# A step takes one query block of all four batches and two pairs of heads

## The chip, the core and the metric

The kernel runs on one core of a Trainium2 chip. Its engines are TensorE (PE in the profile, its weight load PEld), VectorE (DVE), ScalarE (ACT), GpSimd (POOL) and SyncE (SP); each works through its own instructions in order. Here SP issues nearly all transfers between the chip's main memory and its on-chip memory, and sixteen DMA engines carry them out. The metric is the device time of one execution in microseconds (us).

## What is computed

Block-sparse attention over 4 batches, 8 heads, 768 positions in 24 blocks of 32, head size 64, and then a two-layer network over all 3072 positions:

```python
mask = np.abs(blk_i - blk_j) <= 1                       # the block and its two neighbours
mask = mask | (blk_i == 0) | (blk_j == 0) | (blk_i == n_blocks - 1) | (blk_j == n_blocks - 1)
for qb in range(n_blocks):
    for kb in sampled_blocks[qb]:                       # three random blocks for each query block
        mask[qb*block:(qb+1)*block, kb*block:(kb+1)*block] = True
scores = np.where(mask, scale * q @ k^T, -1e9)
attn = softmax(scores);  x = attn @ v                   # then heads side by side: 3072 x 512
h = x @ w_in;  out = (h - np.tanh(h)) @ w_out           # 512 -> 2048 -> 512
```

The first and the last query block see all 768 keys; each of the 22 others sees at most eight blocks: itself and its neighbours, the first, the last, and three sampled ones. The samples are the same in all batches and heads, and known only when the kernel runs.

## The kernel before

**Two stages.** The attention runs first, in 60 units; the network (`FFN`) follows, in 96 units of 512 rows by 128 hidden columns, and its first units overlap the last ones of the attention. Results of the attention go through memory (`xscr`) to the network.

**Units of the attention.** Each unit works on 128 partitions in four quarters of 32 query rows. A batch has 15 units: two pairs Y and X (`kind` "Y", "X"), in which blocks 0 and 23 of four heads go over all keys; ten "group" units, each four query blocks by two pairs of heads; and a "rest" for blocks 21 and 22. The batches follow each other. A unit has `scores` (PE), `most` (row maxima, DVE), `exps` (ACT), `turn` (transposes, PE), `copy` (DVE and ACT), `accum` (weights times V, PE) and `norm` (DVE, then the store of tile x to `xscr` by SP).

**Operands.** `kq` holds K and Q of one batch on chip, two batches at a time; `vnat` holds V of one batch in its natural order for X and Y. For the group units GpSimd copies the sampled columns of K into `kr` (`gather_k`: twelve copies of 128x128 for a group of four blocks, which two units share), and SP fetches rows of V into `vw` (`gather_v`): one transfer for the neighbours of four blocks (96 partitions, 780 KB) and twelve of one sampled block each (32 partitions, 65 KB; a row is 520 numbers, 2080 bytes). The first and last block's rows lie in partitions 96 to 127 and are fetched once a batch for each of the three `vw` buffers.

**What sets the order.** The order is written by hand: every part of unit n is given a time (`at(n + 2.6, accum, u)`), all are sorted, and each engine receives its instructions in that order. `gather_v` of a group stands just behind the `accum` that last read its `vw` buffer, some five units ahead of its own use. SP takes its list in order: a transfer that has to wait holds all behind it. Its transfers use eight completion semaphores in turn (DMAHW0 to DMAHW7 below), and each waits until the transfer eight places ahead of it has landed. Tile x has two buffers, in a pool that it shares with the network's tile u, so the `norm` of a unit writes x only after the store of two units before has landed.

**Weights.** They come as 64-bit words and are turned into 32-bit ones on DVE (`convert_op`); six of the 32 weight tiles are converted during the attention (`load_pre`, `convert_pre`).

Of the kernel before, what the change touches and what calls it, by code (L numbers as in the profile page):

```python
# [44 lines left out]
STEP = 15  # L45
TE = STEP * B + 1.9
LOADK, LOADV, PRE0, DPRE = 1.5, 7.2, 6.1, 6
X0, X1, STAGE = 47, 55.5, (54, 54.5, 56, 56.5)
# [7 lines left out]
NG = 6  # L56
# [37 lines left out]
def attention_ffn(ctx, tc, kq, v, samp, w_in, w_out, rows, out):  # L94
# [3 lines left out]
    xscr = [dpool.tile([S, DM], F32, name=f"xscr{b}") for b in range(B)]  # L98
# [23 lines left out]
class Unit:  # L122


    def __init__(self, n, kind, bt, g, c):
        self.n, self.kind, self.bt, self.g, self.c = n, kind, bt, g, c
        if kind == "group":
            self.quads = [(1 + 4 * g + q, q, None) for q in range(4)]
        elif kind == "rest":
            self.quads = [(21 + q % 2, q % 2, q // 2) for q in range(4)]  # L130
        else:
            self.quads = [((NB - 1) * (q % 2), None, q // 2) for q in range(4)]

    def pair(self, q, half):
        a = self.quads[q][2]
        if self.kind == "group":
            return 2 * self.c + half
        return 2 * (half if self.kind == "rest" else self.c) + a


def attention(ctx, tc, kq, v, samp, w_in, w_out, rows, xscr, ident, banks, mem, px, f2, ffn):
    nc = InOrder(tc)
    att = ctx.enter_context(tc.tile_pool(name="att", bufs=1))
    sm = ctx.enter_context(tc.tile_pool(name="sm", bufs=4))
    sbank, tbank, obank = banks[:4], banks[4:6], banks[6:]

    vw = [att.tile([P, 4, 2, VW], F32, name=f"vw{i}") for i in range(3)]
    kr = [att.tile([P, H // 2, 4, 160], F32, name=f"kr{i}") for i in range(2)]
    wraw = att.tile([P, 1024], I32, name="wraw")
    wtmp = att.tile([P, 256], I32, name="wtmp")  # L150
    vnat = [px.tile([P, 2 * S], F32, tag=("rawx", "rawx", "lo")[i], name=f"vnat{i}")[:, 0 : 2 * VW] for i in range(3)]
    vnat = [t.rearrange("p (t e) -> p t e", t=2) for t in vnat]
    kqs = {}

    def load_kq(bt):
        kqs[bt] = mem.tile([P, H // 2, 2, S], F32, tag=f"A{bt % 2}", name=f"kq{bt}")
        for p in range(H // 2):
            eng = nc.scalar if bt == 0 and p % 2 else nc.sync
            eng.dma_start(out=kqs[bt][:, p], in_=kq[bt][:, p])

    def load_vnat(bt):
        for i in range(3):
            nc.sync.dma_start(out=vnat[i], in_=v[bt][2 * P * i : 2 * P * (i + 1), :].rearrange("(t p) e -> p t e", p=P))
# [27 lines left out]
    def values(eng, x, g, top):  # L191
        n = 12 if g < 5 else 6
        ins, vals = tc.nc.values_load_multi_w_load_instructions(
            x[0:1, 12 * g : 12 * g + n], engines=[eng], min_val=0, max_val=top,
            skip_runtime_bounds_check_because="the samples are clamped into this range on the chip",
        )
        for i in ins:
            tc.keep_in_program_order(i)
        return vals

    def gather_k(bt, g):
        k, to = kqs[bt][:, :, 0, :], kr[g % 2]
        if g < 2:
            for b, c in ((0, 0), (NB - 1, 128)):
                nc.gpsimd.tensor_copy(
                    out=to[:, :, :, c : c + 32], in_=k[:, :, b * 32 : b * 32 + 32].unsqueeze(2).to_broadcast([P, H // 2, 4, 32])
                )
        for i, x in enumerate(values(mybir.EngineType.Pool, kx, g, S - 32)):
            o = 32 + 32 * (i % 3)
            nc.gpsimd.tensor_copy(out=to[:, :, i // 3, o : o + 32], in_=k[:, :, bass.ds(x, 32)])  # L210

    def gather_v(bt, g):
        to, b0, n = vw[g % 3], 1 + 4 * g, 4 if g < 5 else 2
        src = v[bt]
        e = nc.sync
        if g < 3:
            for b, c in ((0, 0), (NB - 1, 1)):
                rows = bass.AP(tensor=src.tensor, offset=src.offset + b * 32 * VW, ap=[[VW, 32], [0, 4], [1, VW]])
                e.dma_start(out=to[96:128, :, c, :], in_=rows)
        l0, l1 = int(g == 0), n - (g == 5)  # L220
        if l1 > l0:
            rows = bass.AP(tensor=src.tensor, offset=src.offset + (b0 + l0 - 1) * 32 * VW, ap=[[VW, 96], [32 * VW, l1 - l0], [1, VW]])
            e.dma_start(out=to[0:96, l0:l1, 0, :], in_=rows)
        if g == 0:
            e.dma_start(out=to[0:32, 0, 0, :], in_=src[S : S + 32, :])
            e.dma_start(out=to[32:96, 0, 0, :], in_=src[32:96, :])
        if g == 5:
            e.dma_start(out=to[0:64, 1, 0, :], in_=src[S - 96 : S - 32, :])
            e.dma_start(out=to[64:96, 1, 0, :], in_=src[S : S + 32, :])
        for i, x in enumerate(values(mybir.EngineType.SP, vx, g, S)):  # L230
            o = 32 * (i % 3)
            e.dma_start(out=to[o : o + 32, i // 3, 1, :], in_=src[bass.ds(x, 32), :])
# [4 lines left out]
    def scores(u):  # L237
        s = sbs[u.n] = sbank[2 * (u.n % 2) : 2 * (u.n % 2) + 2]
        t = kqs[u.bt]
        if u.kind in "XY":  # L240
            o = 0 if u.kind == "X" else 512
            w = 512 if u.kind == "X" else 256
            parts = [(0, slice(0, w), None, slice(o, o + w))]
        else:
            parts = [(h, slice(256 * h + o, 256 * h + o + w), x, None) for h in range(2) for x, o, w in (("w", 0, 96), ("r", 96, 160))]
        for h, cols, what, ks in parts:
            for q in range(4):
                b, l, _ = u.quads[q]
                p = u.pair(q, h)
                for j in range(2):  # L250
                    r = slice(64 * j, 64 * j + 64)
                    if what == "r":
                        rhs = kr[u.g % 2][r, p, l, :]
                    else:
                        rhs = t[r, p, 0, ks or slice(32 * b - 32, 32 * b + 64)]
                    mm(s[j][32 * q : 32 * q + 32, cols], t[r, p, 1, 32 * b : 32 * b + 32], rhs)
# [38 lines left out]
    def accum(u):  # L295
        o = obank[(u.n + (u.kind == "Y")) % 2]
        first = True
        for j in (1, 0):
            for h in (0, 1) if u.kind not in "XY" else (0,):
                chunks = range(2) if u.kind not in "XY" else range(4) if u.kind == "X" else (4, 5)  # L300
                for x, ch in enumerate(chunks):
                    for q in range(4):
                        _, l, _ = u.quads[q]
                        hd = 2 * u.pair(q, h) + j
                        t = pts[u.n, j][:, P * (2 * h + x) + 32 * q : P * (2 * h + x) + 32 * q + 32]
                        e = slice(65 * hd, 65 * hd + 65)
                        r = vnat[ch // 2][:, ch % 2, e] if u.kind in "XY" else vw[u.g % 3][:, l, ch, e]
                        c = slice(65 * (2 * h + j), 65 * (2 * h + j) + 65)
                        last = u.kind != "Y" and x == len(chunks) - 1
                        mm(o[32 * q : 32 * q + 32, c], t, r, start=first and u.kind != "X", stop=last)  # L310
                    first = False

    def norm(u):
# [5 lines left out]
        x = f2.tile([P, 512], F32, tag="u", name=f"x{u.n}")[:, 0 : 64 * n]  # L319
# [3 lines left out]
        to = xscr[u.bt]  # L323
        if u.kind == "group":
            r0 = 32 * (1 + 4 * u.g)
            nc.sync.dma_start(out=to[r0 : r0 + P, 256 * u.c : 256 * u.c + 256], in_=x)
        elif u.kind == "rest":
            for a in range(2):
                nc.sync.dma_start(
                    out=to[672:736, :].rearrange("q (c a d) -> q c a d", c=2, a=2)[:, :, a], in_=x[64 * a : 64 * a + 64].rearrange("q (c d) -> q c d", c=2)  # L330
                )
        else:
            for q in range(4):
                r0, c0 = 32 * u.quads[q][0], P * u.pair(q, 0)
                nc.sync.dma_start(out=to[r0 : r0 + 32, c0 : c0 + P], in_=x[32 * q : 32 * q + 32])
# [6 lines left out]
    at(-9, load_kq, 0)  # L342
    at(-8.9, load_samples)
    at(-8.8, load_vnat, 0)
    units = []
    for bt in range(B):
        for k in range(4):
            units.append(Unit(len(units), "YX"[k % 2], bt, None, k // 2))
        for g in range(5):
            for c in range(2):  # L350
                units.append(Unit(len(units), "group", bt, g, c))
        units.append(Unit(len(units), "rest", bt, 5, None))
    assert len(units) == STEP * B
    for u in units:
        n = u.n
        at(n + 0.3, scores, u)
# [16 lines left out]
    for bt in range(B):  # L373
        n = STEP * bt
        if bt:
            at(n - STEP + LOADK if bt > 1 else -8, load_kq, bt)
            at(n - STEP + LOADV, load_vnat, bt)
        for g in range(NG):
            at(n + 4 + 2 * g - 2.65, gather_k, bt, g)
            at(n + 4 + 2 * g - 2.35 if g > 2 or bt else -5 + g, gather_v, bt, g)  # L380

# [16 lines left out]
    ffn.room(1, mem.tile([P, 8 * S], F32R, tag="A2", name="flat1"))  # L398
    for k in range(2 * NPRE):
        t = PRE0 + DPRE * k  # L400
        at(t, load_pre, k)
        for e in range(2):
            for x in range(3):
                at(t + 2.4 + 1.5 * e + 0.5 * x, convert_pre, k, e, x)
        at(t + 5.12, convert_pre, k, 1, 3)
# [340 lines left out]
```

## Time and profile before

| | us |
|---|---|
| median of three runs (937.07 to 941.82) | 940.14 |
| the profiled execution | 937.58 |
| its span | 935.8 |
| last write of an attention result x | 406.81 |
| from there to the end of the span | 529.0 |

| engine | busy us | share of the span |
|---|---|---|
| PE | 771.4 | 82% |
| PEld | 622.3 | 67% |
| DVE | 566.7 | 61% |
| ACT | 439.5 | 47% |
| POOL | 267.0 | 29% |

The shares are means over two stages that have different limits, so they say little by themselves: the span is read in stretches. An engine's busy time leaves out the issuing of transfers and the waiting on semaphores; a row of a timeline or of the waits names behind "<-" what ended an idle time. KB in a row are units of 1024 bytes.

### The profile page before, as it was taken

To read this page: it belongs to the slowest core of one execution; us is meant where nothing else is said; L and a number is where in the kernel's file an instruction comes from. 1 tells how busy PE (TensorE), PEld (TensorE's weight loads), DVE (VectorE), ACT (ScalarE), POOL (GpSimd) and SP (SyncE) were. 2 spreads that over 40 slices of the span, in tenths; PEclk is the share of its full clock that TensorE was granted. 3 is DMA by queue.
4 is the path that set the end of the run, shared out by engine and by line. 5 is a ranking of instruction groups with operands and counts; after the bars stand their busy time and mean duration, and the time that the engine had idled before them with its cause. 6 is when DMAs were issued, how large, how long until landed. Compare 5 with 4: busy or idle time off the path is not lost.

```text
span 935.8 us, 23960 instructions
## 1 busy us (share of the span) xinstructions
PE 771.4 (82%) x9440; PEld 622.3 (67%) x9440; DVE 566.7 (61%) x1083; ACT 439.5 (47%) x843; POOL 267.0 (29%) x436
## 2 busy tenths in 40 slices
PE   2746855686448666599999999999999999999997
PEld 1535534564337455578888888888888888888886
DVE  3435622465236544469899668777667666766654
ACT  1323422244113342357877755555555555555453
POOL 3112311132113021037787422222222222222222
PEclk9878876688667897999999999999999999999999
DMA  9776576847775576614742110211201110001001
GB/s 353 180 210 154 200 166 149 222 129 231 175 194 133 149 179 181 192 41 135 209 142 89 45 28 8 65 25 26 68 0 17 26 50 1 0 1 46 1 1 45
DMA packets 92725, 99.84 MB, mean 107 GB/s; under 512 B 44995, under 2 KB 60356, under 8 KB 92612
## 3 DMA queue, kind: packets, MB, share of 16 engines
q1 hardware_dynamic: 92180, 96.47, 38.4%
q8 instruction: 74, 1.21, 0.6%
q10 hardware_dynamic: 432, 1.84, 0.5%
q14 instruction: 39, 0.32, 0.1%
HBM read 84.62 MB, written 13.63 MB: 105 GB/s over the span
## 4 chain that ended last, share of the span: by engine, by line
PE 63%; DMA 20%; SPq 8%; DVE 4%; issue 3%; ACT 1%; POOL 0%; DVEq 0%; ACTq 0%; POOLq 0%
PE ps L79 63%; DMA vw<-v 15%; SPq L79 8%; DMA xscr<-x 3%; DVE m L79 1%; DMA vnat<-v 1%; DVE pt L79 1%; DVE nb L79 1%; DVE x L79 0%; ACT p L79 0%; ACT flat L79 0%; DMA flat<-xscr 0%; POOL gl L79 0%; ACT pt L79 0%; DVE rs L79 0%
## 5 line engine op out<-in xcount | busy, mean ns | idle before, releaser
L79 POOL TENSOR_TENSOR gl<-t,gh 128x512 fp32r<-128x512 f32 x96 | 124.7, 1299 | 309.1 <-ACT gh L79 286.8
L79 PE MATMUL ps<-flat,wx 128*128 128x512 f32 x720 | 172.9, 389 | 0.0
L79 ACT ACTIVATE p<-ps,nb 128x256 f32<-128x256 f32 x208 | 89.7, 490 | 161.4 <-DVE nb L79 150.2
L79 PEld LDWEIGHTS ps<-flat,wx 128*128 128x128 f32 x720 | 135.2, 188 | 28.1
L79 ACT ACTIVATE u<-ps 128x512 f32<-128x512 f32 x96 | 57.5, 599 | 198.2 <-PE ps L79 196.3
L79 PE MATMUL ps<-wx,gh 128*128 128x512 f32 x480 | 147.8, 389 | 0.0
L79 PE MATMUL ps<-vw,pt 128*32 128x65 f32 x2816 | 68.8, 252 | 91.5 <-DVE pt L79 88.1
L79 POOL COPY kr<-kq 128x128 f32 (+1 forms) x280 | 73.5, 315 | 215.6 <-PE ps L79 201.8
L79 PEld LDWEIGHTS ps<-vw,pt 128*32 128x32 f32 x2816 | 59.8, 128 | 108.8 <-DVE pt L79 99.9
L79 DVE TENSOR_REDUCE m<-ps 128x2 f32<-128x512 f32 (+2 forms) x120 | 76.5, 649 | 59.8 <-PE ps L79 56.2
L79 DVE TENSOR_TENSOR t<-t,ps 128x512 f32<-128x512 f32 x74 | 50.7, 685 | 86.0 <-ACT t L79 86.0
L79 PEld LDWEIGHTS ps<-wx,gh 128*128 128x128 f32 x480 | 90.1, 188 | 18.6
L79 PE MATMUL ps<-ident,p 128*128 128x128 f32 x448 | 84.5, 347 | 11.1 <-DVE flat L79 4.4
L79 PE MATMUL ps<-wx,gl 128*128 128x512 f32 x240 | 93.4, 389 | 0.0
L79 PE MATMUL ps<-kq 64*32 64x96 f32 (+2 forms) x1664 | 58.1, 336 | 32.2 <-ACT p L79 19.9
L79 DVE TENSOR_TENSOR x<-ps,rs 128x256 f32<-128x256 f32 (+1 forms) x52 | 21.0, 404 | 104.0 <-DMA xscr<-x 102.4
L79 PEld LDWEIGHTS ps<-ident,p 128*128 128x128 f32 x448 | 65.9, 178 | 23.0 <-issue 6.2
L79 DVE COPY_PREDICATED t<-mk,ps 128x512 f32<-128x512 int32 x96 | 71.3, 743 | 7.5 <-DVE ps L79 0.9
L79 ACT ACTIVATE pt<-ps 128x512 f32<-128x512 f32 (+1 forms) x60 | 34.2, 570 | 88.0 <-PE ps L79 87.7
L79 DVE TENSOR_TENSOR ps<-ps,u 128x512 f32<-128x512 f32 x96 | 66.6, 694 | 11.6 <-ACT hs L79 11.5
L79 DVE SCALAR_TENSOR_TENSOR ps<-qq,ps 128x512 f32<-128x512 f32 x96 | 66.6, 694 | 7.7
L79 PE MATMUL ps<-kr,kq 64*32 64x160 f32 x1408 | 55.6, 349 | 18.3 <-issue 18.3
(82 smaller groups left out, 1189.0 us busy)
## 6 DMA issues: line engine op xcount, KB each, us to landing
vw<-v SPq DMA_DIRECT2D x272, 65.0 KB, 3.4
vw<-v SPq DMA_DIRECT2D x16, 780.0 KB, 8.5
kq<-kq SPq DMA_DIRECT2D x14, 768.0 KB, 8.6
stage<-w_in SPq DMA_DIRECT2D x13, 512.0 KB, 3.9
stage<-w_out SPq DMA_DIRECT2D x13, 512.0 KB, 3.3
vnat<-v SPq DMA_DIRECT2D x12, 520.0 KB, 7.3
vw<-v SPq DMA_DIRECT2D x24, 260.0 KB, 4.9
xscr<-x SPq DMA_DIRECT2D x40, 128.0 KB, 2.1
```

The lines of the kernel that those rows point to most:

```text
L79: r = f(*args, **kw)
```

## The change

A unit now takes one query block of all four batches, and two pairs of heads (`c`): the four quarters are the batches. The units of c = 0 come first, then those of c = 1; each half has four pairs Y and X (one for each batch) and 22 "block" units, 60 in all as before. The inputs are laid out for it on the host: K, Q and V by halves of the heads, and a row of V holds all four batches (1040 numbers, 4160 bytes).

- `gather_v` of a unit is one transfer of 96 rows (390 KB), into `vw[i][0]`, and three of 32 rows (130 KB each), into `vw[i][1]`; there are four such pairs of buffers, each for one unit. First and last block's rows are fetched once a half for each (`edges_v`, 130 KB).
- `gather_k` of a unit is three GpSimd copies of 128x256.
- `kq` is loaded by halves, all batches of c = 0 ahead of the first block unit; those of c = 1 during the units of c = 0, and so is `vnat`, now four tiles (rows of 1040 bytes).
- Tile x has a pool of its own with four buffers.
- `xscr` has one tile for each block (32 rows of each batch), so the network takes its rows block by block, and an output tile of 128 rows is stored by four transfers of 32 rows.
- The six early weight tiles are converted from unit 31 on (before: from unit 6 on), since their room is that of the first half's K and Q.

```diff
-STEP = 15
+STEP = 30
-LOADK, LOADV, PRE0, DPRE = 1.5, 7.2, 6.1, 6
-X0, X1, STAGE = 47, 55.5, (54, 54.5, 56, 56.5)
+NVW, NKR, VNAT = 4, 2, T * 260
+LOADK, LOADV, PRE0, DPRE = 9.5, 16, 31, 4
+X0, X1, STAGE = 44, 52, (54, 54.5, 56, 56.5)
...
-    vw = [att.tile([P, 4, 2, VW], F32, name=f"vw{i}") for i in range(3)]
-    kr = [att.tile([P, H // 2, 4, 160], F32, name=f"kr{i}") for i in range(2)]
+    xs = ctx.enter_context(tc.tile_pool(name="xs", bufs=4))
+    vw = [[att.tile([P, B, VW // 2], F32, name=f"vw{i}{x}") for x in range(2)] for i in range(NVW)]
+    kr = [att.tile([P, H, 160], F32, name=f"kr{i}") for i in range(NKR)]
...
+    def gather_v(u):
+        (wa, ra), src, b = vw[u.i % NVW], v[u.c], u.b
         e = nc.sync
...
+        e.dma_start(out=wa[lo:hi], in_=src[32 * b - 32 + lo : 32 * b - 32 + hi])
...
+        for i, x in enumerate(values(mybir.EngineType.SP, vx, b, S)):
+            e.dma_start(out=ra[32 * i : 32 * i + 32], in_=src[bass.ds(x, 32)])
...
-        x = f2.tile([P, 512], F32, tag="u", name=f"x{u.n}")[:, 0 : 64 * n]
+        x = xs.tile([P, 256], F32, tag="x", name=f"x{u.n}")[:, 0 : 64 * n]
...
+        if u.kind == "block":
+            nc.sync.dma_start(out=xscr[u.b][:, 256 * u.c : 256 * u.c + 256], in_=x)
...
+        if u.kind == "block":
+            at(n - NKR + 0.35, gather_k, u)
+            at(n - NVW + 2.65 if u.i >= NVW else -3.5, gather_v, u)
...
-            eng.dma_start(out=self.out[(CT * n + j) * P : (CT * n + j + 1) * P, :], in_=ob)
+            for bt in range(B):
+                r0 = S * bt + BLK * (CT * n + j)
+                eng.dma_start(out=self.out[r0 : r0 + BLK, :], in_=ob[BLK * bt : BLK * bt + BLK])
```

Three places of SP's list show what moved. In the rows, vw, kq, vnat and x are the tiles named above, and the name in square brackets is what the transfer waits for: a semaphore of the eight, or an engine.

The first place is in the middle of the attention, before: the end of one group's fetch, two stores of x and the start of the next fetch.

```order
L79 DMA vw_103<-v 32x520 [waits DMAHW4_49]
L79 DMA xscr_61<-x_2679 128x256 [waits DMAHW5_49,DVE_49]
L79 DMA xscr_61<-x_2775 128x256 [waits DMAHW6_49,DVE_49]
L79 DMA wraw<-w_out 128x1024 [waits DMAHW7_49]
L79 DMA vw_104<-v 96x4x520 [waits DMAHW0_49,PE_49]
L193 TENSOR_LOAD vx
L79 ISA
L79 DMA vw_104<-v 32x520 [waits DMAHW1_49,PE_49]
```

The same place in the changed kernel: the end of one unit's fetch, one store, and the next unit's whole fetch.

```order
L79 DMA vw_133<-v 32x1040 [waits DMAHW1_49]
L79 DMA xscr_64<-x_1251 128x256 [waits DMAHW2_49,DVE_49]
L79 DMA vw_126<-v 96x1040 [waits DMAHW3_49,PE_49]
L193 TENSOR_LOAD vx
L79 ISA
L79 DMA vw_127<-v 32x1040 [waits DMAHW4_49,PE_49]
L79 ISA
L79 DMA vw_127<-v 32x1040 [waits DMAHW5_49]
L79 ISA
L79 DMA vw_127<-v 32x1040 [waits DMAHW6_49]
L79 DMA xscr_65<-x_1402 128x256 [waits DMAHW7_49,DVE_49]
L79 DMA kq_173<-kq 128x3072 [waits DMAHW0_49]
```

Between two stores there stood thirteen fetches of one group, and now stand the four of one unit; K and Q of the second half come between them.

The second place is the head of SP's list, before:

```order
L79 DMA kq_116<-kq 128x1536 x2
L79 DMA si<-samp 1x144
L79 DMA ri<-rows 1x66
L79 DMA vnat_110<-v 128x2x520
L79 DMA vnat_111<-v 128x2x520
L79 DMA vnat_112<-v 128x2x520
L79 DMA kq_149<-kq 128x1536 x4
L79 DMA vw_103<-v 32x4x520 x2
```

And in the changed kernel:

```order
L79 DMA kq_144<-kq 128x1536
L79 DMA si<-samp 1x144
L79 DMA ri<-rows 1x66
L79 DMA vnat_138<-v 128x6x260
L79 DMA kq_144<-kq 128x3072
L79 DMA vnat_139<-v 128x6x260
L79 DMA kq_144<-kq 128x3072
L79 DMA vnat_140<-v 128x6x260
L79 DMA kq_144<-kq 128x3072
L79 DMA vnat_141<-v 128x6x260
L79 DMA vw_126<-v 32x1040
```

K, Q and V of four batches, for half of the heads, now stand ahead of the first fetch into vw; before it was K and Q of two batches and V of one, for all heads.

The third place is SP's end, the stores of the network's last four output tiles (one goes by ACT), before:

```order
L663 DMA out<-ob_0_11596 128x512
L663 DMA out<-ob_1_11599 128x512
L663 DMA out<-stage_6541 128x512
```

And in the changed kernel:

```order
L657 DMA out<-ob_0_10832 32x512 x4
L657 DMA out<-ob_1_10838 32x512 x4
L657 DMA out<-stage_5726 32x512 x4
```

Three stores have become twelve.

## Rows read from the trace of the kernel before

**Rows 1.** The page's slices, 40 of equal length: DMA share and GB/s.

```profile
DMA  9776576847775576614742110211201110001001
GB/s 353 180 210 154 200 166 149 222 129 231 175 194 133 149 179 181 192 41 135 209 142 89 45 28 8 65 25 26 68 0 17 26 50 1 0 1 46 1 1 45
```

**Rows 2.** Busy time by stretch: start:end, length, engines, PEclk, DMA share, GB/s.

```profile
12.40:56.50 44.10, 21.87 (x584) 15.32 (x584) 15.84 (x50) 13.04 (x27) 12.82 (x51) 0.87 0.85 231
57.00:407.00 350.00, 224.09 (x6519) 175.37 (x6520) 165.45 (x443) 113.23 (x256) 66.94 (x235) 0.79 0.66 174
407.00:936.00 529.00, 522.44 (x2306) 430.54 (x2305) 383.85 (x585) 313.24 (x561) 185.47 (x144) 1.00 0.17 47
```

**Rows 3.** The same view, short stretches in which one kind of transfer runs.

```profile
151.50:159.00 7.50, 5.70 (x136) 4.60 (x136) 3.11 (x10) 2.69 (x6) 0.88 (x1) 0.58 1.06 232
159.50:163.00 3.50, 0.00 (x0) 0.00 (x0) 0.00 (x0) 0.00 (x0) 0.00 (x0) 0.74 0.40 101
166.00:170.00 4.00, 3.89 (x72) 3.68 (x72) 2.78 (x9) 0.84 (x2) 0.00 (x0) 0.50 0.99 363
8.00:22.00 14.00, 4.32 (x48) 1.34 (x30) 7.02 (x26) 3.60 (x6) 7.03 (x24) 1.00 1.03 409
```

**Rows 4.** Timeline of SP, two groups: start, length, instruction, count.

```profile
150.11 11.84 SPq L79 DMA_DIRECT2D vw<-v  x15
162.05 2.23 SPq L79 DMA_DIRECT2D xscr<-x  x5
...
165.93 12.28 SPq L79 DMA_DIRECT2D vw<-v  x13
178.31 1.99 SPq L79 DMA_DIRECT2D xscr<-x  x2
...
180.87 4.42 SPq L79 DMA_DIRECT2D vw<-v  x7
```

**Rows 5.** Waits of the engines: who waited for whom, us, times, longest.

```profile
DVE x L79 <- DMA xscr<-x: 102.4, 18, 13.1
...
PE ps L79 <- DVE pt L79: 92.3, 29, 11.5
```

**Rows 6.** Waits of SP's own list, same columns.

```profile
SPq L79 <- DMA vw<-v: 48.8, 32, 3.5
```

**Rows 7.** GpSimd's copies into kr, by form: count, busy us, mean ns, idle.

```profile
L79 POOL COPY kr<-kq 128x128 f32 x264 | 64.5, 297 | 190.1 <-PE ps L79 186.2 <-issue 3.7
...
L79 POOL COPY kr<-kq 128x512 f32<-128x512 f32 x16 | 9.4, 617 | 25.5 <-PE ps L79 15.5 <-DMA kq<-kq 10.0
```

**Rows 8.** Transfers by kind: count, KB each, median us from issue to landing.

```profile
vw<-v SPq DMA_DIRECT2D x272, 65.0 KB, 3.4
vw<-v SPq DMA_DIRECT2D x16, 780.0 KB, 8.5
kq<-kq SPq DMA_DIRECT2D x14, 768.0 KB, 8.6
...
vnat<-v SPq DMA_DIRECT2D x12, 520.0 KB, 7.3
```

**Rows 9.** Timeline of DVE, writes of x: start, length; the last is the attention's last.

```profile
111.03 0.42 DVE L79 TENSOR_TENSOR x<-ps,rs 128x256 f32<-128x256 f32 x1
...
119.49 0.29 DVE L79 TENSOR_TENSOR x<-ps,rs 128x128 f32<-128x128 f32 x1 [0.27 <-DVE rs L79]
...
196.89 0.42 DVE L79 TENSOR_TENSOR x<-ps,rs 128x256 f32<-128x256 f32 x1
...
211.98 0.42 DVE L79 TENSOR_TENSOR x<-ps,rs 128x256 f32<-128x256 f32 x1
...
406.81 0.42 DVE L79 TENSOR_TENSOR x<-ps,rs 128x256 f32<-128x256 f32 x1
```

**Rows 10.** Timeline of SP at the end of the span.

```profile
930.73 0.81 SPq L663 DMA_DIRECT2D out<-ob  x2
931.65 0.38 SPq L663 DMA_DIRECT2D out<-stage  x1
```

More of the change, by code (lines that the diff above doesn't have):

```diff
@@ L55 @@
 VW = H * (D + 1)
-NG = 6
 THR2 = 0.16
@@ L97, in attention_ffn @@
     dpool = ctx.enter_context(tc.tile_pool(name="dpool", bufs=1, space=DRAM))
-    xscr = [dpool.tile([S, DM], F32, name=f"xscr{b}") for b in range(B)]
+    xscr = [dpool.tile([P, DM], F32, name=f"xscr{b}") for b in range(NB)]
     ident = cst.tile([P, P], F32, name="ident")
@@ L122, with __init__, at @@
 class Unit:
[L125 to L138, printed above, removed]
+    def __init__(self, n, kind, c, b, i=None):
+        self.n, self.kind, self.c, self.b, self.i = n, kind, c, b, i
+    def at(self, q, half):
+        if self.kind == "block":
+            return q, self.b, half
+        return self.b, (NB - 1) * (q % 2), q // 2
 def attention(ctx, tc, kq, v, samp, w_in, w_out, rows, xscr, ident, banks, mem, px, f2, ffn):
@@ L189, in load_samples @@
         e.tensor_scalar(out=kx, in0=sf, scalar1=float(BLK), scalar2=None, op0=ALU.mult)
[L191 to L210, printed above, removed]
@@ L212, in gather_v @@
-    def gather_v(bt, g):
-        to, b0, n = vw[g % 3], 1 + 4 * g, 4 if g < 5 else 2
-        src = v[bt]
-        e = nc.sync
[L216 to L232, printed above, removed]
+    vals = {}
@@ new lines, in values, with edges_k @@
+    def values(eng, x, b, top):
+        if b % 4 == 1:
+            ins, vals[eng] = tc.nc.values_load_multi_w_load_instructions(
+                x[0:1, 3 * b - 3 : min(3 * b + 9, 66)], engines=[eng], min_val=0, max_val=top,
+                skip_runtime_bounds_check_because="the samples are clamped into this range on the chip",
+            )
+            for i in ins:
+                tc.keep_in_program_order(i)
+        b = 3 * ((b - 1) % 4)
+        return vals[eng][b : b + 3]
+    def edges_k(c, i):
+        k = kqs[c].rearrange("p b a x s -> p (b a) x s")[:, :, 0, :]
+        for b, o in ((0, 0), (NB - 1, 128)):
+            nc.gpsimd.tensor_copy(out=kr[i][:, :, o : o + 32], in_=k[:, :, b * 32 : b * 32 + 32])
@@ L322, in norm @@
         )
[L323 to L331, printed above, removed]
+        if u.kind == "block":
+            nc.sync.dma_start(out=xscr[u.b][:, 256 * u.c : 256 * u.c + 256], in_=x)
         else:
             for q in range(4):
-                r0, c0 = 32 * u.quads[q][0], P * u.pair(q, 0)
-                nc.sync.dma_start(out=to[r0 : r0 + 32, c0 : c0 + P], in_=x[32 * q : 32 * q + 32])
+                bt, b, p = u.at(q, 0)
+                c0 = P * (2 * u.c + p)
+                nc.sync.dma_start(out=xscr[b][32 * bt : 32 * bt + 32, c0 : c0 + P], in_=x[32 * q : 32 * q + 32])
     ev = []
@@ L552, in fetch_x @@
         raw = self.raw[n, j] = raw if n == 2 and j == 3 else raw.bitcast(F32)
-        b, t = divmod(CT * n + j, T)
-        rows = self.xscr[b][t * P : (t + 1) * P, :]
+        rows = self.xscr[CT * n + j]
         if n < BLOCKED:
@@ L708, in rest @@
         wc = pool("wc")
-        self.tiles += [wc.tile([P, 512], F32R, name=f"wx{i}") for i in range(4 * (NFT - 6))]
+        self.tiles += [wc.tile([P, 512], F32R, name=f"wx{i}") for i in range(4 * (NFT - 6) - 12)]
         for t, f, args in sorted(self.ev, key=lambda e: e[0]):
```

141 lines of the change are left out of this document (79 added, 62 removed).

## The prediction

> **What bounds the kernel now.** I read the slices first [rows 1]: the DMA engines are 0.4 to 0.8 busy in the first 17 or 18 of 40 slices and nearly idle later. Then the busy times by stretch [rows 2]: from 57 to 407 us PE is busy 224 of 350 us and DVE 165, so no engine fills the stretch; from 407 on PE is busy 522 of 529 us. The last attention result is written at 406.81 us [rows 9]. The network behind it is bound by PE, and the change leaves its arithmetic alone; what can move is the attention.
>
> The DMA share there is only 0.66 [rows 2], but the short stretches [rows 3] show two rates of a full queue. Loads to all 128 partitions (kq, vnat) run at 409 GB/s (share 1.03) and 363 (0.99). Fetches into vw run at 232 GB/s with the engines just as full (1.06). Rows of V are 2080 bytes long in vnat and in vw alike, so the lower rate goes with the partitions that are reached (32 or 96), not with the length of a row. And when a group's wide transfer is gone and only its 65 KB pieces are left, the rate is 101 GB/s at share 0.40.
>
> That last figure is SP's own pace: seven issues in 4.42 us [rows 4] are 0.63 us each, and 66.6 kB in 0.63 us are 106 GB/s. So a group costs SP about 12 us (11.84 for fifteen transfers, 12.28 for thirteen) [rows 4], and with its stores 15 to 16 us pass from one group to the next (150.11, 165.93, 180.87), for two units. SP also waits 48.8 us on the landing of earlier vw transfers [rows 6]: with eight semaphores, the ninth transfer waits for the first, and the 780 KB one takes 8.5 us to land [rows 8]. The stores of x stand behind all this; DVE waits 102.4 us for them, and PE 92.3 us for DVE's pt [rows 5], since in DVE's list the copy of pt follows the blocked write of x. PE then frees the vw buffer late, and SP waits again: a ring of waits.
>
> How full is the queue? Fetches into vw are 40,560 KB, or 41.5 MB: 272 pieces and 16 wide ones [rows 8], the rest first and last rows and odd ends. At 232 GB/s they take 179 us. K, Q and V in full (19.0 MB) take 46 us at 409, stores, six weight tiles and early loads of x (11.5 MB) 28 us. Sum 253 us of the 404 from the first load to the last x: 0.63. When SP did nothing but load (12.4 to 56.5 us), the share was 0.85 [rows 2].
>
> **The change part by part.** *Bytes.* A unit fetches 390 + 3 x 130 = 780 KB, just what half a group did. With first and last rows (2 x 1040 KB) the halves make 37.3 MB instead of 41.5.
>
> *Rate.* A row is twice as long, but it goes to the same 32 or 96 partitions. No row shows 4160-byte rows there; the bounds are 232 GB/s (row length does nothing) and 363 (as to 128 partitions). I take 232, because 2080-byte rows reach both rates today.
>
> *SP.* A unit has four fetches and one store. At 0.63 us each these are 3.2 us, against 3.44 us (0.799 MB at 232) that the fetches need and 0.32 for the store; a piece of 133 kB in 0.63 us is 211 GB/s, twice today's pace. So SP no longer starves the queue. Eight transfers in flight are then 1.6 units, 1.5 MB.
>
> *Waits.* Four buffers of x, and a store after every fourth fetch instead of after thirteen, take away what DVE's 102.4 us wait on. The fetch of unit n is released by `accum` of unit n-4, so it has four steps to land. The depth falls from six units to four, but four steps of 4.8 us are 19 us, against landings of 3.4 to 8.5 us [rows 8]. If that cover went, PE would stand by the whole difference in each step.
>
> *Compute.* Where today nothing is late, four steps of DVE's x take 211.98 - 196.89 = 15.1 us, 3.8 each [rows 9]; a conversion falls among them. GpSimd's copies of 256 columns lie between 297 and 617 ns [rows 7], by proportion 404: three are 1.2 us beside a step of 3.8, hidden.
>
> *First half.* K, Q, V of both halves 46.4 us (9.5 MB at 409 each), vw 18.64 MB at 232: 80.3 us, stores 3.15 MB: 7.7 us; sum 134.4. With the queue 0.9 full (above today's load-only 0.85, since the pieces are wider) 149 us, from 2 us on: it ends at 151. The first block unit needs 23 us of loads to be through, where the four pairs of Y and X run meanwhile.
>
> *Second half.* Four pairs Y and X, nearly free of fetches. One pair took 8.46 us [rows 9], partly behind another unit; four take 30. Then 22 units of 3.44 + 0.32 us, and weights and x (5.2 MB) 0.58 us each: 4.34, at 0.9 4.82. The first four are fetched during the pairs and take 3.8. So 22 x 4.82 - 4 = 102. The last x falls at 151 + 30 + 102 = 283 instead of 407: **-124 us**.
>
> *Network.* 529 us as before. The end costs more: its three SP stores are now twelve. They start at 930.73 and the last is issued at 931.65 [rows 10]; twelve at 0.40 (two took 0.81) put the last at 935.1, **+3.5**. The other 84 added stores and issues lie under PE work; uncovered they would be 0.4 us each.
>
> Sum: 937.6 - 124 + 3.5 = 817 for the profiled execution; the median of the runs lies 2.6 above it, so **820**.
>
> [...] The row says 232 GB/s for partitions 0 to 95 with a full queue [rows 3]. [...]
>
> **The rivals.** (1) *The fetch stops being the limit.* The wider transfers reach up to 363 GB/s. A unit's queue time is then 2.2 + 0.32 + 0.58 = 3.1 us, under the 3.8 of compute. First half (46.4 + 51.4 + 7.7) / 0.9 = 117, pairs 30, then 22 units at 4.1 (3.8 and DVE's conversions, now all here) 90: last x at 237, 771 + 3 = 774. For it: 363 with rows of 2080 bytes; against: 232 with rows of the same length to the partitions that stay.
>
> (2) *The queue stays as empty as now*, 0.63: PE's clock (0.79 in this stretch [rows 2]), the order of SP's list or another wait takes the place of the ring. First half 215, pairs 30, 22 x 6.9 = 152: last x at 397, 931 + 3 = 934, near no change. Against it: x's buffers, SP's halved issues.
>
> (3) *Slower: the landing of transfers decides.* Eight in flight and five transfers a unit mean a step of 5/8 of the landing time. To reach 407 again with 30 us of front loads and 30 of pairs, a step must be 7.9 us, so a landing 12.6 us; at 14 us the last x is at 445 and the time 979. For it: 780 KB takes 8.5 us and 768 KB 8.6 [rows 8], and kq now comes in 1.5 MB loads between the fetches. Against: those are four among some hundred, and the common piece is 130 KB.
>
> That the change would not do what it says is excluded by the order of SP's list, which shows four fetches between two stores.
>
> **How the numbers follow.** Forecast 0.60, rival (1) 0.20, (2) 0.14, (3) 0.06. The forecast's own range goes from a full queue (first half 136, 30, 22 x 4.34: last x 260, time 797) to a queue 0.77 full (860). With (1) the range is 770 to 860 and leaves 0.2 out. A measurement of this kernel can tell about 0.5%, 5 us, from no change. Forecast, (1) and two thirds of (2) are faster: 0.90; the rest of (2) 0.04 is the same; slower 0.06.
>
> **What would show it.** Right: DMA share 0.9 or more and about 230 GB/s in the fetches from 50 to 150 us; DVE's wait for stores of x below 20 us; steps near 4.8 us; last x near 283; from there 532 us to the end. Wrong: fetches above 300 GB/s with a step of 3.8 (rival 1), a share near 0.65 with a new name at the top of the waits (2), landings over 10 us of the 130 KB pieces (3), or a network longer than 535 us, which I have put at no cost.

## The result, and the profile after

The changed kernel takes 871.08 us (median of four runs, 862.02 to 874.05) against 939.26 for the kernel before (four runs beside it): a ratio of 0.9257 [0.9184, 0.9329], 68 us faster. The forecast was 120 us faster, 820, and its range ended at 860. So the sign was right, the size was little more than half of it, and the range was missed.

The profiled execution took 874.05 us, its span is 872.3. The page's slices (the granted clock of TensorE in tenths, the DMA share, GB/s), which answer to [rows 1], its line on the chain that ended last, its line on the queue that carries instructions, and three lines of its transfers (count, KB each, median us to landing):

```profile
PEclk9987878999989899999999999999999999999999
DMA  9879988447968941564202121112111100010001
GB/s 354 233 192 292 277 235 196 132 120 189 246 182 242 246 112 56 159 183 155 95 9 57 21 49 25 26 26 42 30 17 26 44 13 1 1 28 22 1 1 48
...
q8 instruction: 74, 1.21, 0.6%
...
PE 76%; issue 9%; DVE 7%; SPq 3%; DMA 2%; ACT 2%; DVEq 0%; POOL 0%; ACTq 0%
...
vw<-v SPq DMA_DIRECT2D x152, 130.0 KB, 4.7
vw<-v SPq DMA_DIRECT2D x40, 390.0 KB, 6.5
...
xscr<-x SPq DMA_DIRECT2D x44, 128.0 KB, 5.1
```

The busy stretch of the DMA engines is shorter and fuller: of its slices nine are at 0.8 or more, two before. "issue", 9% of the chain, is time in which an engine waited for nothing that the profile shows. Waits of the engines and of SP's list, which answer to [rows 5, 6]:

```profile
PEld ps L79 <- issue: 106.0, 146, 5.2
...
PE ps L79 <- issue: 64.2, 30, 5.0
...
PE ps L79 <- DVE pt L79: 10.0, 11, 2.4
...
SPq L79 <- PE ps L79: 62.7, 42, 4.7
SPq L79 <- DVE x L79: 31.3, 13, 5.5
...
SPq L79 <- DMA vw<-v: 16.4, 21, 1.6
```

The ring of waits is gone: DVE's wait for the stores of x (102.4 us before) no longer appears, PE's for `pt` fell from 92.3 to 10.0, SP's for earlier fetches from 48.8 to 16.4. SP now waits for PE, which frees the buffers. And PE's own first wait has become one without a name, 64.2 us; before, it was 28.2.

Stretches (columns as in [rows 2]; from 2 to 175 us is the first half) and four writes of x by DVE, which answer to [rows 9]: the first block unit's, the last one of the first half, the last pair's, and the attention's last.

```profile
50.00:100.00 50.00, 35.03 (x1052) 27.93 (x1052) 25.72 (x64) 15.99 (x37) 8.74 (x24) 0.81 0.89 266
100.00:150.00 50.00, 36.09 (x1127) 29.36 (x1134) 25.66 (x64) 18.58 (x43) 8.74 (x24) 0.78 0.91 222
50.00:175.00 125.00, 89.36 (x2852) 71.02 (x2852) 67.87 (x173) 44.38 (x103) 19.66 (x54) 0.84 0.82 222
...
206.00:330.00 124.00, 87.25 (x2891) 69.09 (x2890) 76.27 (x198) 51.12 (x117) 24.97 (x58) 0.90 0.75 196
330.00:872.30 542.30, 531.04 (x2307) 430.50 (x2305) 383.74 (x585) 313.04 (x561) 185.64 (x144) 1.00 0.18 46
...
2.00:175.00 173.00, 116.33 (x3584) 87.97 (x3584) 90.69 (x243) 61.32 (x137) 25.34 (x70) 0.88 0.85 241
...
100.00:106.00 6.00, 3.79 (x131) 3.09 (x131) 2.15 (x6) 2.17 (x5) 1.09 (x3) 0.78 1.06 232
132.00:138.00 6.00, 3.04 (x126) 2.39 (x110) 3.13 (x8) 2.11 (x5) 1.09 (x3) 1.00 1.07 228
```

```profile
53.84 0.42 DVE L79 TENSOR_TENSOR x<-ps,rs 128x256 f32<-128x256 f32 x1
...
174.70 0.42 DVE L79 TENSOR_TENSOR x<-ps,rs 128x256 f32<-128x256 f32 x1
...
206.18 0.29 DVE L79 TENSOR_TENSOR x<-ps,rs 128x128 f32<-128x128 f32 x1
...
329.86 0.42 DVE L79 TENSOR_TENSOR x<-ps,rs 128x256 f32<-128x256 f32 x1
```

Set against the forecast's terms, with two experiments beside it that are told below (all from such rows):

| | forecast | after | no fetch | fewer PE instructions, no fetch |
|---|---|---|---|---|
| first half ends at, us | 151 | 174.7 | 150.2 | 135.7 |
| four pairs Y and X | 30 | 31.5 | 31.8 | 32.7 |
| 22 units of the second half | 102 | 123.7 | 98.4 | 92.4 |
| last x to the end of the span | 532.5 | 542.4 | 540.9 | 541.2 |

The differences to the forecast are 23.7, 1.5, 21.7 and 9.9 us: 57, which is 874 less the 817 of the sum. Two things are to be explained: both halves of the attention are some 22 us too long, and the network 10.

### The profile page after: what moved, and what is told of

It reads as the page before. It is cut to its first block, busy times and chain, and to the rows that moved or that the text cites. A ratio compares the mean times of both kernels' runs of the same rounds, so it can differ in the third digit from the quotient of the medians.

```text
span 872.3 us, 23289 instructions
## 1 busy us (share of the span) xinstructions
PE 755.5 (87%) x9440; PEld 601.9 (69%) x9440; DVE 571.7 (66%) x1083; ACT 440.1 (50%) x843; POOL 244.8 (28%) x296
## 3 DMA queue, kind: packets, MB, share of 16 engines
q8 instruction: 74, 1.21, 0.6%
## 4 chain that ended last, share of the span: by engine, by line
PE 76%; issue 9%; DVE 7%; SPq 3%; DMA 2%; ACT 2%; DVEq 0%; POOL 0%; ACTq 0%
PE ps L79 76%; SPq L555 3%; DVE m L79 3%; DVE nb L79 1%; DVE pt L79 1%; DMA si<-samp 1%; DVE ps L79 1%; ACT p L79 1%; DMA wraw<-w_in 1%; DMA stage<-w_in 0%; DVE x L79 0%; DVE t L79 0%; DVE s L79 0%; DVE flat L79 0%; DMA xscr<-x 0%
## 5 line engine op out<-in xcount | busy, mean ns | idle before, releaser
L79 PE MATMUL ps<-flat,wx 128*128 128x512 f32 x504 | 124.3, 395 | 0.8 <-DVE t L79 0.8
L79 POOL COPY kr<-kq 128x256 f32 (+1 forms) x140 | 51.0, 405 | 223.3 <-PE ps L79 197.9
L79 PEld LDWEIGHTS ps<-flat,wx 128*128 128x128 f32 x504 | 94.5, 188 | 23.9 <-DVE t L79 1.2
L79 PE MATMUL ps<-wx,gh 128*128 128x512 f32 x336 | 105.3, 394 | 0.0
L79 PE MATMUL ps<-ident,p 128*128 128x128 f32 x448 | 72.3, 309 | 19.4 <-DVE pt L79 8.7
L79 PE MATMUL ps<-flat,gh 128*128 128x512 f32 x288 | 88.9, 390 | 0.0
L79 PE MATMUL ps<-vw,pt 128*32 128x65 f32 x2816 | 60.4, 243 | 25.6 <-issue 21.4
L79 PEld LDWEIGHTS ps<-ident,p 128*128 128x128 f32 x448 | 56.0, 157 | 30.6 <-issue 12.2
L79 PEld LDWEIGHTS ps<-kq 64*32 64x32 f32 x1664 | 29.4, 116 | 66.4 <-issue 40.1
L79 PEld LDWEIGHTS ps<-wx,gh 128*128 128x128 f32 x336 | 63.1, 188 | 15.2
L79 ACT ACTIVATE pt<-ps 128x512 f32<-128x512 f32 (+1 forms) x60 | 34.1, 569 | 74.7 <-PE ps L79 73.8
L79 PE MATMUL ps<-flat 128*128 128x512 f32 x288 | 69.8, 391 | 1.2 <-ACT pt L79 0.7
```

The costliest lines, as they stand in the source:

```text
L79: r = f(*args, **kw)
```

## The experiments

**What the stalls look like.** Three neighbouring stretches of the changed kernel, and PE's timeline in them (start, length, operation, count, idle time before it):

```profile
290.00:296.00 6.00, 3.98 (x144) 3.15 (x141) 3.94 (x10) 2.18 (x6) 2.54 (x5) 1.00 0.97 269
296.00:302.00 6.00, 1.59 (x41) 1.21 (x47) 1.89 (x6) 2.12 (x5) 0.00 (x0) 0.77 0.99 220
302.00:308.00 6.00, 4.93 (x117) 3.88 (x101) 3.13 (x8) 2.09 (x5) 1.09 (x3) 0.67 0.90 279
```

```profile
295.61 1.09 PE L79 MATMUL ps<-ident,p 128*128 128x128 f32 x8
296.63 0.38 PE L79 MATMUL ps<-kq 64*32 64x96 f32 x11
301.42 0.38 PE L79 MATMUL ps<-kq 64*32 64x96 f32 x3 [4.41 <-issue]
```

PE stops for 4.41 us in the middle of one run of scores, after eleven matmuls that read the same tile as the twelfth. The profile names nothing that the twelfth waits for. Others stop in a run of weights times V (4.39 us at 97.42). The granted clock falls from full speed to a mean of 0.77 and 0.67 in the stretch of the stop and the one behind it: by single microseconds it is 1.00 up to 299 us, 0.60 in the next, and 0.50 in each of the six from 300 to 306.

PE and PEld run 9440 instructions each, and the queue q8 brings 74 pieces of 1.21 MB together, 16 KB each: one for 255 of these instructions, about one for a unit, which has 272. In the trace's records of this queue a piece landed at 299.82 us, and at 82.49, 96.06 and 103.11; PE went on at 301.42, 84.06, 97.42 and 104.46, each time 1.4 to 1.6 us later. The place of the stops says more. Counted over all records of PE in the trace (the 18,880 instructions and 114 others), 26 stops of over 1 us stand exactly where 449 and a multiple of 256 of them have been run: the stops lie whole pieces apart, and PE goes on 1.2 to 1.9 us after the next piece has landed. The 26 make 63.7 us, nearly all of the 64.2.

So theory **P**: PE runs dry of its own instructions, whose pieces go through the same DMA engines as the fetches (the page counts q8's packets on the sixteen engines too, 0.6% of their time), and the fuller these are, the later they come. Rivals: **D**, rows of V land late; **C**, an instruction on PE costs time whatever the DMA engines do. The expectations take C in two ways: first as PE's clock, low for reasons of its own, and with fewer instructions as PE's own busy time.

**No fetch.** V is fetched for the first four units alone; later ones meet wrong rows of V.

```diff
-            at(n - NVW + 2.65 if u.i >= NVW else -3.5, gather_v, u)
+            if u.i < NVW:
+                at(-3.5, gather_v, u)
```

> Leaves out every fetch into vw after those of the first four block units, so the later units multiply stale rows of V; all else stays. Three theories for the steps of 5.6 to 5.8 us in the block units. (P) PE runs dry of its own instructions, which come through the same DMA engines in 16 KB pieces, and a piece comes late when these are full: with the engines nearly idle PE's waits that the profile calls issue fall from 64 to under 15 us, the step to about 3.8, the time to about 790. (D) PE waits for rows of V that land late, and the profile does not name it: the same here, 790. (C) PE's clock, low for reasons of its own, sets the step: step over 5, time over 860.

**Fetched, but unread.** Every fetch goes out as before, into buffers that PE doesn't read (it takes the first unit's rows of V throughout).

```diff
-        (wa, ra), src, b = vw[u.i % NVW], v[u.c], u.b
+        (wa, ra), src, b = vw[1 + u.i % 3 if u.i else 0], v[u.c], u.b
...
-                        r = vnat[bt][:, ch, e] if u.kind in "XY" else vw[u.i % NVW][ch][:, bt, e]
+                        r = vnat[bt][:, ch, e] if u.kind in "XY" else vw[0][ch][:, bt, e]
```

> Every fetch into vw is made as in the changed kernel, but from the second unit on into buffers that PE never reads; PE multiplies the first unit's rows throughout, so no unit needs a fetch to have landed, and the DMA engines are as full. (P) instructions come late: the issue waits stay at 50 us or more, step 5 or more, time 855 to 880. (D) rows of V come late: issue waits under 15 us, step 3.8, time about 790. (C) as P in time, but with few issue waits.

**Half the fetch, unread.** The same without the 390 KB transfer of each unit after the first.

> Leaves out, after the first unit, the transfer of the neighbours' rows, so that a unit fetches 390 instead of 780 KB of V, and reads V from the first units' buffers throughout (so the weights meet wrong rows of V). Everything PE executes is as in the changed kernel. Theory P (PE's own instruction pieces come late in measure with the load of the DMA engines): between no fetch and all fetches, so PE's issue waits 35 to 50 us (30.1 with no fetch, 62.8 with all unread), last x at 295 to 315, 838 to 858 us. Rival D2 (the number of queued transfers holds PE's pieces up, not their bytes): three of four transfers stay, so the waits stay above 55 us and the time above 862. Rival (nothing to do with the load, only chance): anything, with last x unrelated to the waits.

| | us | last x at | PE's issue waits, us (times) | DMA share, PEclk in 50:175 |
|---|---|---|---|---|
| after | 874.05 | 329.9 | 64.2 (30) | 0.82, 0.84 |
| fetched, unread | 870.63 | 327.8 | 62.8 (33) | 0.82, 0.86 |
| half, unread | 832.73 | 289.3 | 36.6 (33) | 0.64, 0.95 |
| no fetch | 823.02 | 280.3 | 30.1 (28) | 0.39, 0.96 |

The rows of fetched-unread, a stretch and a wait:

```profile
50.00:175.00 125.00, 88.18 (x2868) 68.57 (x2858) 67.66 (x173) 45.13 (x105) 19.67 (x54) 0.86 0.82 222
...
PE ps L79 <- issue: 62.8, 33, 4.4
```

D falls: with no row of V needed by anyone the time stays. C as the clock falls too (it gave over 860 us with no fetch; the run took 823), and so does the number of transfers as the cause (over 55 us of waits with half the fetch; they are 36.6). What lengthens PE's steps is that the DMA engines are full, and on these points, one run each, it grows steeply only near full: by the last x, a DMA share of 0.64 costs 9 us over one of 0.39, a share of 0.82 another 38.5. P had expected a more even rise: with half the fetch the waits came as it forecast, but the last x and the time below its ranges.

The stops of over 1 us at the end of a piece follow: 26 (63.7 us) after, 25 (60.1) fetched but unread, 13 (25.2) with half, 11 (22.7) with no fetch. The records also show that the pieces come later, if PE's queue asks for one at the same place each time. The network suggests that it does: there, where the engines are nearly idle (a share of 0.18 after), a piece begins to move when PE is 152 to 195 instructions past a multiple of 256. In the attention (from 45 us on) it begins, in the median, 4.2 us after PE has begun the 160th, 3.9 unread, 2.6 with half and 2.5 with no fetch; the move itself takes no longer (median 1.07 us both after and with no fetch).

With no fetch the waits stay above the 15 us that P had expected at most, and so does the time: PE runs dry with light engines too.

**Rows of 2080 bytes.** The same rows, laid into the buffer in two pieces.

> The same rows of V, fetched as two pieces of 2080 bytes each (the length before the change) into buffers with a gap between the halves; counts of transfers, bytes and waits as in the changed kernel. If the long rows make a piece of instructions wait longer at its DMA engine, issue waits fall from 64 towards 30 us and the time to 840 to 850. If it is only how full the engines are, no change: 862 to 876. If row length had raised the fetch rate, it would fall below 230 GB/s and the time rise by over 10 us.

870.38 us, last x at 323.7, issue waits 62.1; 224 GB/s at a share of 0.85 from 50 to 175 us, where the changed kernel has 222 at 0.82. The length of a row changed neither the rate at a given share, within some 3%, nor the waits (62.1 us against 64.2).

**Fewer PE instructions.** The scores of 96 and 160 columns become one matmul of 256; GpSimd lays the neighbours' columns into `kr` beside the sampled ones (room for the wider `kr` is made by putting the early weights' raw words into tiles of the network). A unit has 208 PE instructions instead of 272 and computes the same.

```diff
+        nc.gpsimd.tensor_copy(out=kr[u.i % NKR][:, :, 0:96], in_=k[:, :, 32 * u.b - 32 : 32 * u.b + 64])
...
-            parts = [(h, 256 * h + o, w, None) for h in range(2) for o, w in ((0, 96), (96, 160))]
+            parts = [(h, 256 * h, 256, None) for h in range(2)]
```

> GpSimd copies the 96 window columns of K beside the others (a fourth copy, about 0.9 us a unit), so that one product of 256 columns takes the place of two (96 and 160): 32 products of scores a unit instead of 64, some 208 PE instructions with their weight loads instead of 272; bytes of V and all waits as they are. (P) the supply of instructions sets the step: it falls with their count, 5.7 x 208/272 = 4.4, which over 44 units is 55 us, time 815 to 835. (D) rows of V set the step: no change, 862 to 874. (C) PE's own busy time falls by some 0.5 us a unit: 840 to 855.

847.92 us (844.29 to 850.53), ratio 0.8962 [0.8911, 0.9012]. Its queue of instructions and its waits:

```profile
q8 instruction: 63, 1.03, 0.6%
...
PE ps L79 <- issue: 34.5, 22, 4.1
...
PE ps L79 <- DMA vw<-v: 7.2, 7, 1.9
```

2816 instructions less are 11 pieces less, and the last x comes at 304.3, 25.6 us sooner. The time lies in C's range and not in P's, but not for C's reason: PE's busy time fell by 5.8 us (755.5 to 749.7), where C had 0.5 us a unit, 22 in all, while its issue waits fell by 29.7 and the stops at the end of a piece from 26 to 11 (26.4 us). What P left out is the next limit: from 50 to 160 us the DMA share is now 0.93, and where a row of V is late, the profile says so.

**Fewer PE instructions, no fetch.** Both edits at once, to tell P from C.

> Two edits at once: 208 instead of 272 PE instructions in a unit, and no fetch of V after the first four units (left out, so the weights meet wrong rows of V). Theory P (what lengthened PE's steps is its own instructions, late while the DMA engines are full): with the engines light, fewer instructions gain little, since their pieces come in time: last x at 265 to 278 against 280.3 with no fetch alone, PE's issue waits 18 to 28 us, time 806 to 821. Rival (an instruction costs PE time of its own, whatever the DMA engines do): the gain is the same as with all fetches on, 23 us: last x at 257, time below 802.

803.76 us, last x at 260.8:

```profile
q8 instruction: 63, 1.03, 0.5%
...
PE ps L79 <- issue: 13.7, 9, 5.0
```

Neither forecast is met: P's ranges begin at 265 and 806, the rival's numbers are 257 and below 802. P had said that with light engines fewer instructions gain little. They gain 19.5 us (280.3 to 260.8) where they gain 25.6 with full ones. Issue waits fell by 16.4 and PE's busy time by 8.7 (738.7 to 730.0), while its waits for `pt` rose by 6.8; the stops at the end of a piece fell from 11 to 5 (10.2 us). So C holds in the sense that an instruction had a price with light engines too, and most of this price was the piece that it came in, not its own busy time. Full DMA engines put 43 to 50 us on top (304.3 - 260.8, 329.9 - 280.3).

Where in the engines' queues a piece stands before it moves isn't in the records. Of the 49.6 us between after and no fetch, issue waits are 34.1, and PE's busy time is 16.8 longer (755.5 against 738.7), with the granted clock at 0.84 against 0.96 from 50 to 175 us; the two make up the difference. That the clock falls because of the stops is argued from the stretches shown above.

**Two buffers of x**, in place of four, in the changed kernel; and **three in the kernel before**, in place of two.

```diff
-    xs = ctx.enter_context(tc.tile_pool(name="xs", bufs=4))
+    xs = ctx.enter_context(tc.tile_pool(name="xs", bufs=2))
```

> The changed kernel with two buffers of x instead of four. If the four buffers carry a good part of the gain, DVE's wait for stores of x comes back (over 40 us) and the time rises by 20 us or more, to over 890; if the wider fetches alone shorten the stores' place in SP's list, 868 to 880.

> The kernel before with three buffers of x instead of two, nothing else. If the ring of waits through x was what held the attention back, DVE's wait for stores of x falls from 102 us to under 50 and the time by 20 us or more, to below 920. If the fetch of a group (12 us of SP's list for two units, at twelve pieces of 65 KB) was the bound, the wait only moves elsewhere and the time stays within 8 us of 940.

The first took 881.82 us; DVE's wait for a store of x was 15.4 us (three times), nearly all of it 13.6 us ahead of the block units; the time is a little above the second alternative's. The second took 935.94 (ten runs, 933.46 to 943.4), a ratio of 0.9934 [0.9908, 0.9961]. Its waits:

```profile
PE ps L79 <- DVE pt L79: 83.5, 26, 10.6
DVE x L79 <- DMA xscr<-x: 66.8, 15, 10.3
```

In the kernel before, a buffer more took 36 us out of the 102.4 us wait and 7 us out of the time: the wait was the form that SP's slow fetch took. Of the gain of 68 us x's four buffers carry some 10, by one run, which is less than the 12 us between the lowest and the highest run of the changed kernel. The rest lies in the other parts of the change; that it is the wider transfers is argued from SP's rows, since no run has them alone.

**Tiles of 1600 numbers.** In the changed kernel PE's matmuls on the network's `wx` weights take 394 ns instead of 389, and a step of the network that uses them 5.59 us instead of 5.44. `VNAT` is 1560 there, and the tiles behind are moved by it: in the built programs `wx` starts 192 bytes past a multiple of 256 before, and 64 after. With 1600 it is 192 again. (Past a multiple of 128, which the expectation names, it is 64 in all three.)

```diff
-NVW, NKR, VNAT = 4, 2, T * 260
+NVW, NKR, VNAT = 4, 2, 1600
```

> One number: VNAT 1600 instead of 1560, so that the tiles of the network's later weights start 64 bytes further into each row of on-chip memory than a multiple of 128, as all of them did before the change, where the changed kernel has them at other offsets. In the changed kernel the network's steps on those weights take 5.59 us instead of 5.44. If the place of the weights is the cause, all steps are 5.44 again and the stretch from the last x to the end falls from 542 to about 534 us. If it is something else (the order of x in memory, the added stores), it stays at 542. The attention stays as it is.

From the last x to the end 535.7 us instead of 542.4. The page's group of after, and of this kernel:

```profile
L79 PE MATMUL ps<-wx,gh 128*128 128x512 f32 x336 | 105.3, 394 | 0.0
```

```profile
L79 PE MATMUL ps<-wx,gh 128*128 128x512 f32 x336 | 103.5, 389 | 0.0
```

That is 6.7 of the network's 9.9 us. Other runs agree: with tiles of 1560 and the stores as in the changed kernel, eight runs take 540.9 to 544.9 us from the last x to the end, with 1600 three take 535.7 to 537.6. The attention of this run was 8.6 us shorter too (last x at 321.3), which the edit doesn't touch; runs with this attention end it between 321 and 330.

**The third chunk's x.** SP, after: the second chunk's sixteen stores, and behind them the fetch of the third chunk's x.

```profile
455.96 3.65 SPq L657 DMA_DIRECT2D out<-ob  x8
459.71 4.76 SPq L657 DMA_DIRECT2D out<-stage  x8
464.56 20.45 SPq L555 DMA_DIRECT2D stage<-xscr  x32
485.44 10.64 SPq L555 DMA_DIRECT2D xn<-xscr  x16
```

Three steps of the network, which end at about 489 to 502 us, take 6.31, 5.95 and 7.52 us there; before, 5.44 each. Three cures were tried, the last two upon fewer PE instructions and 1600 together.

```diff
-            for bt in range(B):
-                r0 = S * bt + BLK * (CT * n + j)
-                eng.dma_start(out=self.out[r0 : r0 + BLK, :], in_=ob[BLK * bt : BLK * bt + BLK])
+            r0 = BLK * (CT * n + j)
...
+                to = bass.AP(tensor=self.out.tensor, offset=self.out.offset + r0 * DM, ap=[[S * DM, B], [DM, BLK], [1, DM]])
+                eng.dma_start(out=to, in_=ob)
```

> An output tile goes out as one transfer over the four batches again, except the last four tiles. If the added stores on SP's list delay the third chunk's x, PE's wait of 3.5 us near the 30th network unit goes away and the stretch from the last x to the end falls from 542 to about 538 us. If it is the reading of x by blocks, nothing changes.

One store for four: 873.25 us, 546.9 from the last x. DVE's waits for that x are 8.9 and 1.4 us instead of 4.4 and 2.5. SP has fewer issues, but waits for earlier stores to land (4.9 us for one of `ob`, 3.4 for one of `stage`; in the changed kernel it has no such wait there), and comes to the block of x fetches at 464.02, no sooner: 139.4 us behind the last x, where the changed kernel has 134.7.

> The changed kernel with both remedies: 208 instead of 272 PE instructions in a unit, and the tiles wx 1600 instead of 1560 numbers wide, which brings the network's weights back to their places of before. If the two gains add: 848 minus 4 to 7, so 840 to 845 us, with network steps of 5.44 and from the last x to the end 536 to 540. If merging has itself moved the weights so that they already stand well or badly elsewhere: 846 to 850. Against the kernel before a ratio of 0.889 to 0.897.

Fewer PE instructions and 1600 together: **839.53 us** (five runs, 837.35 to 843.96), ratio 0.8899 [0.8860, 0.8937], 537.6 from the last x (544.5 without the 1600). The two gains add, 8.4 us where 4 to 7 were forecast. Of the kernels that leave nothing out it is the fastest.

> As the one before, and the stores of the output tiles ob of each chunk (those of 128 partitions that leave from f2's buffers, eight transfers) go by ACT's queue instead of SP's, so that SP comes to the fetch of the third chunk's x some 3.65 us earlier. If the lateness of that x is the length of SP's list: the three long steps at units 29 to 31 lose 3 to 4 us, 837 to 842. If the lateness is the landing of the stores whose room it takes: no change within 1.5 us. If ACT's eight issues at 0.4 us delay PE's next steps: up to 3 us more.

Half of the stores by ACT: 852.41 us (851.2 to 854.01). ACT's timeline at the second chunk's stores:

```profile
428.92 1.78 ACTq L79 DMA_DIRECT2D out<-ob  x4
430.75 0.60 ACT L79 ACTIVATE ob<-ps 128x512 f32<-128x512 f32 x1 [1.86 <-PE ps L79]
431.38 1.98 ACTq L79 DMA_DIRECT2D out<-ob  x4
433.40 0.63 ACT L79 ACTIVATE gh<-t 128x512 fp32r<-128x512 f32 x1 [2.06 <-issue]
```

The issues stand in ACT's list ahead of `gh`, for which PE waits: one step of 7.4 to 8.8 us at each chunk. The x comes no sooner either (two steps of 9.02 and 8.38), and the whole is 13 us longer, outside all three forecasts.

> As the combination of merged scores and 1600-wide tiles, but the first tile of the third chunk's x is fetched into the free third part of its stage tile, some fifteen transfers ahead of the second chunk's stores (in place of the third tile, which stood there). If the lateness is SP's list behind the sixteen stores, the first tile no longer waits (5.1 us of DVE's waits go) and only the last tile's is left: units 29 to 31 take 3 to 6 us less, 834 to 838 us. If the last tile's arrival sets the end of it whatever comes first: no change, 839 to 841.

The first tile's fetch put ahead of the stores: 843.04 us (842.11 to 848.37), no gain. DVE's first look at each tile of that x:

```profile
451.00 0.72 DVE L79 STREAM_TRANSPOSE ps<-stage 128x512 f32<-128x512 f32 x1
454.22 0.72 DVE L79 STREAM_TRANSPOSE ps<-stage 128x512 f32<-128x512 f32 x1
459.20 0.72 DVE L79 STREAM_TRANSPOSE ps<-stage 128x512 f32<-128x512 f32 x1
470.52 0.73 DVE L79 STREAM_TRANSPOSE ps<-xn 128x512 f32<-128x512 f32 x1 [6.56 <-DMA xn<-xscr]
```

The first three are on time, and the last one, whose fetch ends SP's list as before, costs all that the others had cost: one step of 11.59 us in place of three long ones. The sixteen stores are 8.4 us of SP's list where four were 2.3, and SP comes to the block of x fetches 134.7 us behind the last x where it was 130.9 before. That this is what the x is late by is argued: in neither kernel with fewer stores on SP's list did SP come to the fetches sooner, so no run has tested it.

## Why the prediction was right and where it was wrong

**The bound before and the ring: right.** SP's pace starved the DMA engines (a share of 0.66 from 57 to 407 us); with the wider fetches it is 0.82 from 50 to 175 us, and the three named waits fell (to none, 10.0 and 16.4 us). A third buffer of x alone, in the kernel before, gave 7 us of the 68.

**The rate: right.** It is 232 and 228 GB/s with full engines in stretches of mainly fetches (share 1.06 and 1.07), with rows twice as long, as in [rows 3].

**DMA share from 50 to 150 us: right** (0.89 and 0.91 forecast as 0.9 or more), **but the step "0.9 full" was wrong for a half.** From 50 to 175 it is 0.82, in the second half 0.75.

**The step that failed is the compute step: "four steps of DVE's x take 15.1 us, 3.8 each", taken as what PE and the others need whatever the queue does.** I let the longer of two times count, 4.34 us of queue (4.82 at 0.9) over 3.8 of compute, as if they were independent. A unit takes 5.76 us in the first half (53.84 to 174.70, 21 units) and 5.62 in the second, and no data is late: PE runs dry of its own instructions. Even with no fetch at all a unit takes 4.57 and 4.47, so 3.8 was too low by some 0.7 with the queue out of the way; 3.76 comes in the first half alone, with fewer PE instructions and no fetch. That the halves with no fetch come to 150 and 98 us, near the sum's 151 and 102, is luck: the sum had them from a queue that is full, which it isn't there. With full engines PE loses 43 to 50 us more. The price was in sight: before, PE had 28.2 us of waits that the profile calls issue, with the engines two thirds full (11 stops at the end of a piece, 23.8 us), and I forecast that they would be full without asking who else uses them.

The traces show the pieces (74 of 16 KB for 18,880 instructions of PE and PEld, and stops 256 instructions apart or a multiple of that), and that their fetch is not hidden: the stops at the end of a piece are 22.7 us with no fetch of V and 63.7 after.

**A second term was too small: the queue of the first half, 134.4 us.** From 2 to 175 us the share is 0.85, which is 147 us of full engines. In part this is a slip in reading [rows 3]: 232 and 409 GB/s stand there at shares of 1.06 and 1.03, and I took them as what a share of 1 moves (some 6 us). At 0.9 the 147 us would end at 165 instead of 151, and with fewer PE instructions, at 0.93 from 50 to 160 us, the first half does end at 164.4. So by an estimate from these shares some 14 of its 23.7 us lie in this term, and the rest in engines that were less full while PE stood still.

**The network at no cost: wrong by 10 us.** I had named a network longer than 535 us as a sign of error. The width of `vnat`'s tiles moved the weights (6.7 us), a part of the change that I hadn't looked at; and "the other 84 added stores and issues lie under PE work" seems not to hold for twelve of them, behind which one fetch of x comes late (3.5 us; the link is argued). The end's +3.5 was near: from ACT's first work on the last unit to the end of the span it is 16.5 us instead of 13.6. Had the network been as forecast, 861 would still be outside the range, by 1 us.

**The rivals.** None came true as told. "The queue stays as empty as now" named PE's clock or another wait that takes the ring's place, and something like it came: the time ended 51 us above the forecast, where that rival had 114. Late landings (130 KB in 4.7 us) decided nothing.

## What to carry to other kernels

When a change fills the DMA engines, ask what else goes through them. Here it was PE's own instructions, 74 pieces of 16 KB, and PE's unnamed waits were the first sign in the profile of before (28.2 us, and 64.2 after). Then fewer, wider instructions on that engine paid too (871 to 848 us, with the same arithmetic). A tile's new width moves what is placed behind it; compare the mean ns of untouched matmuls in both profiles (389 and 394 here), since 5 ns in each of a thousand are 5 us.

## What was not expected of the hardware

- PE stopped for up to 5.0 us in mid-run with nothing named, always at the end of a piece of 256 instructions, and resumed 1.2 to 1.9 us after the next 16 KB piece had landed: 26 stops and 63.7 us with full DMA engines (a share of 0.82 from 50 to 175 us), 13 and 25.2 with half the fetch (0.64), 11 and 22.7 with none (0.39).
- A 128x512 matmul took 394 ns with the network's weights 64 bytes past a multiple of 256, and 389 with them at 192. Which property of the place counts isn't settled.
- Rows of 2080 and 4160 bytes were fetched into 32 and 96 partitions at nearly the same rate (224 GB/s at a share of 0.85 and 222 at 0.82), and the kernel took the same time (870.38 and 871.08 us).
